# Logits of the last block from gate-times-second-layer weights, its second layer moved into the routing round

## The chip, the cores and the metric

The kernel runs on one core of a Trainium2 chip. The metric is device time in microseconds (us) of one launch. The engines are TensorE (PE, with its weight loads PEld), VectorE (DVE), ScalarE (ACT), GpSimd (POOL), and SyncE (SP), which here issues most of the transfers.

## The reference

Attention over 8 batches and heads of 576 tokens gives x of 4608 tokens by 512. A two-layer network, a gate with a greedy assignment of tokens to 8 experts of 576 places each, and the experts follow:

```python
h = x @ w_in                      # 512 -> 2048
g = h - np.tanh(h)
x = g @ w_out                     # 2048 -> 512
logits = x @ w_gate               # 4608 x 8
flat = logits.flatten()
order = np.argsort(-flat)         # best (token, expert) pairs first
for idx in order:                 # a token takes its best expert that has a place left
    tok, e = (int(idx) // E, int(idx) % E)
    if assigned[tok] >= 0 or counts[e] >= cap:
        continue
    assigned[tok] = e
    counts[e] += 1
for e in range(E):
    mask = assigned == e
    h = np.maximum(x[mask] @ w1[e], 0.0)
    out[mask] = h @ w2[e]
```

All products are made with each operand split into a high and a low part of the fp32r type, three products for one (high by high, low by high, high by low).

## The kernel before, in words

The first part, `phase_ab`, goes over 12 blocks (n = 0 to 11) of 384 tokens. A block has 16 steps (f = 0 to 15), one for each 128 columns of the 2048. From block 2 on the steps come in a fixed order that the loop at the end of `phase_ab` writes out. In step s:

- `h_mm` (L421) gives TensorE 12 products of 128x384 into one of two h banks in PSUM;
- `act1` (L460) gives ScalarE four operations (S, t, T, m) and VectorE four (`act_do`, L448 to L457) that make t = h - tanh h; the last of them frees the h bank;
- `act2` (L473) of the step before splits t into gh (ScalarE) and gl (GpSimd, L471);
- `attn_...` give the attention of a later block, in three parts that take turns by step;
- `logit` (L525) takes a few logits of the block before on VectorE: one operation for each token group of 128 and expert, `scalar_tensor_tensor` of the x2 row and the expert's gate column, summed into a column of L. 24 make a block; the table LOGITS says how many a step takes;
- `x2_mm` (L479) gives TensorE nine products of 128x512 of step s-2 into three x2 banks.

At f = 15, `x_split` splits the attention's result for the next block, half on GpSimd and half on VectorE. After step 15's x2 products `x2_out` (L497) copies the three banks to SBUF and SP stores them to `x2d` in DRAM. Each engine does its queue in the order in which the code gives it instructions.

For block 0, and after the loop for block 11, the logits come from `tlogit` (L534) in place of VectorE: four transposes of the x2 row on TensorE, a copy to SBUF, four fp32 products with the gate, a copy to L.

The second part, `phase_c`, makes eight rounds: a round picks an expert and its tokens (`route`, on VectorE with small products on TensorE), loads that expert's weights, gathers the tokens from `x2d` (GpSimd, L1097), and computes. The round for one expert runs beside the products of the one before; round 0 runs alone. Its first instruction needs all of L; its products (`rt`) need VectorE's comparison (cmp) before each. In it EI is the expert's number and IDX the tokens' places. When EI is known SP loads eight tiles of 256 KB of w1 (`load_w1`, L1059), ScalarE and GpSimd split them (L1074, L1075: w1h, w1l). `run`, near the end, sets what of routing, weights and tokens is given out in which order before the first expert.

Of the kernel before, what the change touches and what calls it, by code (L numbers as in the profile page):

```python
# [39 lines left out]
LOGITS = ((0, 0, 0, 0, 3, 2, 1, 3, 2, 1, 3, 2, 3, 3, 1, 0), (0, 0, 0, 0, 0, 4, 0, 0, 3, 2, 4, 3, 2, 3, 2, 1))  # L40
# [12 lines left out]
MSB = 1  # L53
# [10 lines left out]
PA, PB = C0 / KSC ** 2, C1 / KSC ** 4  # L64

# [61 lines left out]
def moe_kernel(ctx, tc, qkv, wio, wgt, wgk, ident, w1, w2, qtab, vtab, amask, cint, rtf, rti, rth, rtb, out):  # L127
# [5 lines left out]
    L = cpool.tile([128, NCOL, E], F32, name="L")  # L133

    with ExitStack() as bs:
        phase_ab(tc, bs, qkv, wio, wgt, wgk, ident, qtab, vtab, amask, cint, x2d, L)
    with ExitStack() as cs:
        phase_c(tc, cs, w1, w2, rtf, rti, rth, rtb, x2d, L, out)


def phase_ab(tc, ctx, qkv, wio, wgt, wgk, ident, qtab, vtab, amask, cint, x2d, L):
    nc = tc.nc
    wpool = ctx.enter_context(tc.tile_pool(name="wpool", bufs=1))
# [3 lines left out]
    psA = ctx.enter_context(tc.tile_pool(name="psA", bufs=3, space=PSUM))  # L147
    psH = ctx.enter_context(tc.tile_pool(name="psH", bufs=2, space=PSUM))
    psX = ctx.enter_context(tc.tile_pool(name="psX", bufs=3, space=PSUM))
# [130 lines left out]
    def attn_scores():  # L280
# [3 lines left out]
        if early(k):  # L284
            pool, tag = (psX, "x2") if k < 4 and k % 2 == 0 else (psA, "psa")
            PSA[k] = [pool.tile([128, 512], F32, tag=tag, name=f"ps{i}") for i in range(3)]
# [53 lines left out]
    def warm(n):  # L340

        z = bw.tile([128, 512], BF16, tag="S", name="z")
        nc.vector.memset(z, 0.0)
        ps = psX.tile([128, 512], F32, tag="x2", name="warm")
        for _ in range(n):
            nc.tensor.matmul(ps, z[:, :128], z, start=True, stop=True)
# [74 lines left out]
    def h_mm(s):  # L421
        n, f = seq[s]
        h = psH.tile([128, 512], F32, tag="h", name="h")
# [42 lines left out]
    def g_high(s):  # L466
        G[s] = [bw.tile([128, TB], F32R, tag=f"g{i}", name=f"g{i}") for i in "hl"]
# [11 lines left out]
    def x2_mm(s, part=None):  # L479
        n, f = seq[s]  # L480
        if f == 0 and part != 1:
            pool, tag = (psA, "psa") if n == 1 else (psX, "x2")
            X2[n] = [pool.tile([128, DM], F32, tag=tag, name="x2") for _ in range(NT)]
# [13 lines left out]
    def x2_out(n):  # L497
        rs = []
        for i in range(NT):
# [5 lines left out]
            if n >= NB - 2 and i == 1:  # L505
# [4 lines left out]
            if n in (0, NB - 1):  # L510
# [23 lines left out]
    def tlogit(c, r, xT, idm, wk, tp, dve=False):  # L534
# [3 lines left out]
        if dve:  # L538
            nc.vector.tensor_copy(out=xT, in_=tp)
        else:  # L540
            nc.scalar.activation(xT, tp, AF.Copy)
# [4 lines left out]
        nc.vector.tensor_copy(out=L[:, c, :], in_=tp[:, :E])  # L546


# [110 lines left out]
    _, idm, wk = tmp  # L659
    nc.gpsimd.memset(ST[64:], 0.0)  # L660
    PB_ = [psA.tile([128, 512], F32, tag="psa", name=f"pb{i}") for i in range(3)]
# [8 lines left out]
    for s in range(NJ + 2, NS + 2):  # L670
        n, f = seq[s] if s < NS else (NB, s - NS)
        part = au(s)
        if s < NS:
            h_mm(s)
            if n == 2 and f in (3, 5, 8):
                next(tl, None)
                if f == 8:
                    gate(0)
            if n == 2 and f in (2, 4, 7):
                c, r = pl.pop(0)  # L680
                tl = tlogit(c, r, bw.tile([128, DM], F32, tag="junk", name="xT", bufs=1), idm, wk, PB_[2])
                next(tl)
            if f == NF - 1 and n + 1 < NB:
# [13 lines left out]
            if head and f == 1:  # L697
                act2(s - 1)
            act1(s)
        if 1 <= s <= NS and not (s < NS and head and f == 1):  # L700
            act2(s - 1)
        if part == 0:
# [8 lines left out]
        logit((LOGITS[n == 2])[f])  # L711
        if n == NB - 1 and f == 0:
            idm, wk = qt[:, 0, :], qt[:, 1, :KC * E]
            nc.sync.dma_start(out=idm, in_=ident)
            nc.sync.dma_start(out=wk, in_=wgk)
        if s >= 2 and (s >= NS or not head):
            x2_mm(s - 2)
    logit(100)
# [585 lines left out]
```

## Time and profile before

| what | value |
|---|---|
| median of 3 runs | 1524.99 us (1524.97 to 1526.43) |
| the profiled execution | 1528.85 us, of which the span is 1527.0 |
| TensorE busy | 1447.8 us, 95% of the span |
| VectorE busy | 1075.0 us, 70% |
| ScalarE busy | 780.6 us, 51% |
| GpSimd busy | 542.2 us, 36% |

Of 40 equal slices of the span, TensorE is busy 90% or more in all but the first, the last and three around the routing's round 0 (8, 2 and 8 tenths, 954 to 1069 us). The granted clock is at 0.9 or more in every slice but the 27th, from 993 to 1031 us, where it shows 0.5; a slice averages, so the stretch itself is read below. A share says how much of a stage an engine works, and not what the stage waits for: that is read from a stretch's own rows. In the rows "[6.65 <-DVE P L863]" means that the engine was idle for 6.65 us before this instruction, and that what ended it was VectorE's instruction on P of line 863.

### The profile page before, as it was taken

To read this page: it belongs to the slowest core of one execution; us is meant where nothing else is said; L and a number is where in the kernel's file an instruction comes from. 1 tells how busy PE (TensorE), PEld (TensorE's weight loads), DVE (VectorE), ACT (ScalarE), POOL (GpSimd) and SP (SyncE) were. 2 spreads that over 40 slices of the span, in tenths; PEclk is the share of its full clock that TensorE was granted. 3 is DMA by queue.
4 is the path that set the end of the run, shared out by engine and by line. 5 is a ranking of instruction groups with operands and counts; after the bars stand their busy time and mean duration, and the time that the engine had idled before them with its cause. 6 is when DMAs were issued, how large, how long until landed. Compare 5 with 4: busy or idle time off the path is not lost.

```text
span 1527.0 us, 26098 instructions
## 1 busy us (share of the span) xinstructions
PE 1447.8 (95%) x9500; PEld 1271.5 (83%) x9500; DVE 1075.0 (70%) x2682; ACT 780.6 (51%) x1616; POOL 542.2 (36%) x487
## 2 busy tenths in 40 slices
PE   7999999999999999999999999828999999999997
PEld 5787889898989898899888988717788888887996
DVE  5777757787878878788878787777676766765210
ACT  6899965555555646565655555413332323423421
POOL 3555621212222212121222122234544625537541
PEclk9999999999999999999999999959999999999999
DMA  8432131111111111111020100122432432425210
GB/s 280 164 106 97 56 134 70 63 44 62 42 63 42 61 44 42 63 38 67 22 78 27 65 1 21 38 73 72 135 118 87 142 110 81 138 92 186 87 63 32
DMA packets 48609, 122.42 MB, mean 80 GB/s; under 512 B 6624, under 2 KB 13408, under 8 KB 48224
## 3 DMA queue, kind: packets, MB, share of 16 engines
q1 hardware_dynamic: 41184, 99.80, 19.3%
q0 software_dynamic: 6144, 19.93, 4.1%
q8 instruction: 75, 1.23, 0.3%
q10 hardware_dynamic: 1152, 1.02, 0.2%
q14 instruction: 54, 0.44, 0.1%
HBM read 101.85 MB, written 18.87 MB: 79 GB/s over the span
## 4 chain that ended last, share of the span: by engine, by line
PE 75%; ACT 8%; DVE 7%; issue 4%; DMA 2%; POOL 2%; SPq 0%; POOLq 0%; ACTq 0%; DVEq 0%
PE x L490 22%; PE h L427 21%; PE ff L1189 12%; PE ff L1158 11%; PE pb L291 2%; PE pb L358 2%; PE pb L370 1%; DMA wst<-in_wio 1%; ACT wst L213 1%; ACT t L440 1%; PE tp L1112 1%; ACT wst L218 1%; PE pb L306 1%; POOL w2l L1075 1%; DVE t L451 1%
## 5 line engine op out<-in xcount | busy, mean ns | idle before, releaser
L471 POOL TENSOR_TENSOR gl<-t,gh 128x384 fp32r<-128x384 f32 x192 | 197.2, 1027 | 633.1 <-ACT gh L468 566.3
L427 PE MATMUL h<-xh,w0h 128*128 128x384 f32 x704 | 238.6, 339 | 1.8 <-DVE t L457 1.8
L437 ACT ACTIVATE S<-h 128x384 f32<-128x384 f32 x192 | 93.4, 487 | 283.4 <-PE h L427 283.4
L427 PE MATMUL h<-xh,w0l 128*128 128x384 f32 x704 | 236.8, 336 | 0.0
L490 PE MATMUL x<-w1h,gh 128*128 128x512 f32 x576 | 232.0, 403 | 2.7 <-ACT gh L468 2.7
L490 PE MATMUL x<-w1l,gh 128*128 128x512 f32 x576 | 227.1, 394 | 0.2 <-DVE w1l L238 0.2
L490 PE MATMUL x<-w1h,gl 128*128 128x512 f32 x576 | 217.3, 395 | 1.4 <-POOL gl L471 0.8
L451 DVE SCALAR_TENSOR_TENSOR t<-t,S 128x384 f32<-128x384 f32 x192 | 114.2, 595 | 141.1 <-ACT t L440 140.3
L531 DVE SCALAR_TENSOR_TENSOR junk<-x2r,wg 128x512 f32<-128x512 f32 x240 | 167.0, 696 | 5.1
L427 PE MATMUL h<-xl,w0h 128*128 128x384 f32 x704 | 151.7, 336 | 0.3 <-DVE xl L414 0.3
L427 PEld LDWEIGHTS h<-xh,w0h 128*128 128x128 f32 x704 | 131.9, 187 | 11.5 <-DVE t L457 3.3
L1075 POOL TENSOR_TENSOR w2l<-ws,w2h 128x512 fp32r<-128x512 f32 x64 | 82.5, 1291 | 163.7 <-ACT w2h L1074 163.7
L427 PEld LDWEIGHTS h<-xh,w0l 128*128 128x128 f32 x704 | 132.1, 188 | 7.1
L490 PEld LDWEIGHTS x<-w1h,gl 128*128 128x128 f32 x576 | 108.4, 189 | 29.1 <-POOL gl L471 5.7
L1189 PE MATMUL ff<-w2h,hh 128*128 128x512 f32 x320 | 128.1, 400 | 3.1 <-DVE hl L1171 2.0
L490 PEld LDWEIGHTS x<-w1h,gh 128*128 128x128 f32 x576 | 108.5, 188 | 26.0 <-ACT gh L468 4.0
L457 DVE COPY_PREDICATED t<-m,h 128x384 f32<-128x384 uint16 x192 | 114.5, 596 | 21.3 <-ACT m L446 2.6
L1189 PE MATMUL ff<-w2l,hh 128*128 128x512 f32 (+1 forms) x320 | 128.0, 400 | 0.6 <-POOL w2l L1075 0.6
L440 ACT ACTIVATE t<-S,bias 128x384 f32<-128x384 f32 x192 | 118.2, 616 | 17.1 <-POOL gl L471 1.1
L427 PEld LDWEIGHTS h<-xl,w0h 128*128 128x128 f32 x704 | 125.7, 188 | 0.9 <-DVE xl L414 0.9
L490 PEld LDWEIGHTS x<-w1l,gh 128*128 128x128 f32 x576 | 108.6, 189 | 17.8 <-DVE w1l L238 0.5
L1158 PE MATMUL ff<-xh,w1h 128*128 128x288 f32 x512 | 115.5, 304 | 6.4 <-DVE hl L1171 5.5
(210 smaller groups left out, 2935.3 us busy)
## 6 DMA issues: line engine op xcount, KB each, us to landing
ws<-in_w SPq DMA_DIRECT2D x128, 256.0 KB, 2.9
ain<-in_qkv SPq DMA_DIRECT2D x36, 768.0 KB, 4.1
wst<-in_wio SPq DMA_DIRECT2D x32, 512.0 KB, 3.5
x2d<-x2r SPq DMA_DIRECT2D x33, 256.0 KB, 2.0
w1h<-in_qkv SPq DMA_DIRECT2D x12, 192.0 KB, 4.8
w1l<-in_qkv SPq DMA_DIRECT2D x12, 192.0 KB, 3.5
w0h<-in_qkv SPq DMA_DIRECT2D x12, 192.0 KB, 4.5
w0l<-in_qkv SPq DMA_DIRECT2D x12, 192.0 KB, 4.3
```

What stands on the lines that cost most here:

```text
L291: nc.tensor.matmul(PSA[k][a][:, chunk(c)], kt[r, chunk(c)], q[r, chunk(c)], start=True, stop=True)
L427: nc.tensor.matmul(h[:, :TB], w[0][f][:, hp, :], x, start=i == 0, stop=i == 11)
L437: nc.scalar.activation(S, h, AF.Square, scale=KSC)
L440: nc.scalar.activation(AT[s][2], AT[s][1], AF.Square, bias=bias[:, 0:1])
L451: nc.vector.scalar_tensor_tensor(t, t, PA - PB * PB / 4, S, op0=OP.add, op1=OP.mult)
L457: nc.vector.copy_predicated(t, m.bitcast(U16), h)
L471: nc.gpsimd.tensor_tensor(G[s][1], TT.pop(s), G[s][0].bitcast(F32), op=OP.subtract)
L490: nc.tensor.matmul(X2[n][i], g[:, i * 128:i * 128 + 128], w, start=(f == 0 and g is gh and w is wh), stop=(f == NF - 1 and g is gl))
L531: nc.vector.scalar_tensor_tensor(j, r, 1.0, wg[e // 4][:, e % 4, :], op0=OP.mult, op1=OP.mult, accum_out=L[:, c, e:e + 1])
L1075: nc.gpsimd.tensor_tensor(l, s, h.bitcast(F32), op=OP.subtract)
L1158: nc.tensor.matmul(ps[u], w[:, k, :], x[:, k, 288 * u:288 * u + 288], start=i == 0, stop=i == 11)
L1189: nc.tensor.matmul(o, h, w, start=f == 0 and i == 0, stop=f == 7 and i == len(prods) - 1, skip_group_check=t == 4)
```

## The change

Logits are x2 times the gate, and x2 is g times w_out. The new kernel makes WP = w_out times gate (2048 x 8) while earlier blocks run, and takes the logits of the last block as g times WP, without its x2. The x2 of that block is still needed by the gathers, and its products are given out later.

- WP. Its 16 pieces are one for each f. Ten pieces are made on VectorE (`w_gate`, eight operations a piece, placed by the table GATES in steps f = 14, 15 and 0 to 3 from block 2 on), from a sum of the high and low weight tiles that GpSimd makes (`w_add`). Six pieces (WPE) are made by TensorE in blocks 3 to 8: GpSimd's sum `wt` at f = 12, four transposes right behind h of f = 13, a copy on ScalarE, four fp32 products at f = 14, and a copy. In block 10 WP is split in two parts, WPS.
- Last block, from f = 2. `logit_mm` gives three products of 72x384 a step, of step s-3, into one bank. Three h banks take turns in place of two. x2 products are taken from a generator (`x2_rest`, 144 products): 17 by FILL0 in the block, 23 by FILL1 behind it, and the remaining ones by FILL2 in round 0, ahead of the routing's products. The g tiles stay in the places of weights that are no longer used.
- Block 10's logits: two token groups by `tlogit` in the last block, the third by eight operations on VectorE.
- The last logits are copied (lT), transposed three times and copied to L.
- The copies of the last x2 are all on ScalarE, and its stores on SP come behind the loads of w1.
- The routing's tables are loaded in block 2 and its state is copied in block 11. Pools of PSUM become fixed banks, and the weights of `phase_c` take the places of earlier tiles.

The core of the diff:

```diff
-LOGITS = ((0, 0, 0, 0, 3, 2, 1, 3, 2, 1, 3, 2, 3, 3, 1, 0), (0, 0, 0, 0, 0, 4, 0, 0, 3, 2, 4, 3, 2, 3, 2, 1))
+LOGITS = ((0, 0, 0, 0, 3, 2, 1, 3, 2, 1, 3, 2, 3, 3, 1, 0), (0, 0, 0, 0, 0, 4, 0, 0, 3, 2, 4, 3, 2, 3, 2, 1),
+          (0, 0, 0, 0, 1, 1, 1, 1, 1, 1, 1, 1, 0, 0, 0, 0))
+WPE = 10, 11, 12, 13, 14, 15
+GATES = 1, 3, 2, 1, 0, 0, 0, 0, 0, 0, 0, 0, 0, 0, 2, 2
+FILL0 = 0, 0, 0, 0, 1, 1, 1, 1, 1, 1, 2, 2, 2, 2, 2, 1
+FILL1 = 2, 8, 6, 4, 2
+FILL2 = 3, 7, 2, 2, 2, 6, 0, 9, 0, 9, 0, 10, 0, 9, 0, 9, 0, 9, 7, 10, 5, 8, 200
...
-        h = psH.tile([128, 512], F32, tag="h", name="h")
+        h = bank((3, 4, 1)[f % 3] if n == NB - 1 else 3 + s % 2, "h")
...
+    def w_add(o, f):
+
+        h, l = (w[1][f].rearrange("p k m -> p (k m)").bitcast(F32) for w in (WH, WL))
+        nc.gpsimd.tensor_tensor(o, h, l, op=OP.add)
+
+    def w_gate(k):
+
+        f, e = divmod(k, E)
+        j = bw.tile([128, DM], F32, tag="junk", name="junk", bufs=1)
+        nc.vector.scalar_tensor_tensor(j, wsum, 1.0, wg[e // 4][:, e % 4, :], op0=OP.mult, op1=OP.mult,
+                                       accum_out=WP[:, k:k + 1])
+
+    def logit_mm(s, part):
+
+        f = seq[s][1]
+        gh, gl = G[s]
+        for i, g in ((0, gh), (1, gh)) if part == 0 else ((0, gl),):
+            nc.tensor.matmul(lg[:MG, :TB], WPS[:, i, E * f:E * f + MG], g, start=f == 0 and part == i == 0,
+                             stop=f == NF - 1 and part == 1)
+
+    def x2_rest():
+
+        n, s0 = NB - 1, NS - NF
+        X2[n] = [bank(i + 5, "x2") for i in range(NT)]
+        order = [(f, i) for f in range(NF - 3) for i in range(NT)]
+        order += [(f, i) for i in range(NT) for f in range(NF - 3, NF)]
+        for f, i in order:
+            gh, gl = G[s0 + f]
+            wh, wl = (w[1][f].rearrange("p k m -> p (k m)") for w in (WH, WL))
+            for j, (g, w) in enumerate(((gh, wh), (gh, wl), (gl, wh))):
+                nc.tensor.matmul(X2[n][i], g[:, i * 128:i * 128 + 128], w, start=f == j == 0, stop=f == NF - 1 and j == 2)
+                if f == NF - 1 and j == 2:
+                    c = n * NT + i
+                    r = wpool.tile([128, DM], F32, tag=TAGS[32 + i], name="x2r")
+                    nc.scalar.activation(r, X2[n][i], AF.Copy)
+                    nc.sync.dma_start(out=x2d[c * 128:c * 128 + 128, :], in_=r)
+                yield
...
+            if n - 3 in range(len(WPE)) and f in (13, 14):
+                if f == 13:
+                    tl = tlogit(WP[:, E * wf:E * wf + E], wt, wt, idm, wk, PB_[2])
+                next(tl, None)
...
+            if end:
+                if f == 2:
+                    lg = bank(2, "lg")
+                if f >= 3:
+                    logit_mm(s - 3, 0)
+                    logit_mm(s - 3, 1)
+                fill(FILL0[f])
...
+        if NG < nd and (n, f) > (2, 12):
+            for _ in range(GATES[f]):
+                w_gate(NG)
+                NG += 1
+                if NG % E == 0:
+                    due = NG < nd
+                    break
+        if n - 3 in range(len(WPE)) and f == 12:
+            wf = WPE[n - 3]
+            wt = ap_.tile([128, 2, 3, 128], F32, tag="ms", name="wt", bufs=MSB).rearrange("p a c t -> p (a c t)")[:, :DM]
+            w_add(wt, wf)
...
-    tls = [tlogit(c, r, xT, idm, wk, PB_[i], i != 1) for i, ((c, r), xT) in enumerate(zip(pl, spare))]
-    for _ in range(2):
-        for t in tls:
-            next(t, None)
+    for i, k in enumerate(FILL1[:3]):
+        fill(k)
+        logit_mm(NS - 3 + i, 0)
+        if i == 2:
+            fill(FILL1[3])
+        logit_mm(NS - 3 + i, 1)
+    lT = sp[:MG, 2 * DM:2 * DM + TB]
+    nc.scalar.activation(lT, lg[:MG, :TB], AF.Copy)
+    fill(FILL1[4])
...
     def run(i, done):
         while not done():
             next(threads[i][1])
+            if i == 0:
+                fill_(next(pauses, 0))
```

TensorE's queue in block 3 at f = 13, with the change: h's last products (L449), the transposes of wt (L562), x2 of step 11 (L515).

```order
L449 MATMUL h<-xl,w0h_1760 128x384 x4
L562 MATMUL pb_2271<-tab_65,wt 128x128 [waits DMAHW2_49,DVE_49,Pool_49]
L562 MATMUL pb_2271<-tab_65,wt 128x128 x3
L515 MATMUL x_3233<-w1h_1703,gh 128x512 [waits Activation_49]
L515 MATMUL x_3233<-w1l_1710,gh 128x512
```

Before, x2 of step 11 followed h directly; the transposes now stand between, and wait for GpSimd.

TensorE's queue where the last block ends, before: products of `tlogit` (L544) and then the routing's first products (L930).

```order
L544 MATMUL pb_2268<-qt,xT 128x8 [waits DMAHW3_49,DVE_49]
L544 MATMUL pb_2268<-qt,xT 128x8 x3
L544 MATMUL pb_2269<-qt,xT 128x8 [waits Activation_49]
L544 MATMUL pb_2269<-qt,xT 128x8 x3
L544 MATMUL pb_2270<-qt,xT 128x8 [waits DVE_49]
L544 MATMUL pb_2270<-qt,xT 128x8 x3
L930 LDWEIGHTS cmp_10375 [waits DVE_49,PE_49]
L930 MATMUL rt<-P,cmp_10375 128x32 [waits DVE_49]
```

And with the change: the last logit product (L588), the transposes of lT (L850), then 22 x2 products (L601), of which the first and the last stand here, and the routing's first product (L1053).

```order
L588 MATMUL lg<-gl,wps 72x384 [waits Pool_49]
L601 MATMUL x_10006<-w1l_950,gh 128x512
L601 MATMUL x_10006<-w1h_932,gl 128x512
L850 MATMUL lt<-tab_65,sp 128x72 [waits DVE_49,Activation_49]
L850 MATMUL lt<-tab_65,sp 128x72 x2
L601 MATMUL x_10007<-w1h_932,gh 128x512
...
L601 MATMUL x_10008<-w1h_1159,gh 128x512
L1053 LDWEIGHTS cmp_10501 [waits DVE_49,PE_49]
L1053 MATMUL rt<-P,cmp_10501 128x32 [waits PE_49]
```

The x2 products that stood ahead of the logits now stand behind them, ahead of the routing's.

SP's queue in round 0, with the change: the last two loads of w1 (L1186), the three stores of the last block's x2 (L606), then the loads of w2 (L1191).

```order
L1186 DMA ws<-in_w 128x512 [waits DMAHW0_49]
L1186 ISA
L1186 DMA ws<-in_w 128x512 [waits DMAHW1_49]
L606 DMA x2d<-x2r 128x512 [waits DMAHW2_49,Activation_49]
L606 DMA x2d<-x2r 128x512 [waits DMAHW3_49,Activation_49]
L606 DMA x2d<-x2r 128x512 [waits DMAHW4_49,Activation_49]
L1191 ISA
L1191 DMA ws_11092<-in_w 128x512 [waits DMAHW5_49,PE_49,Pool_49]
```

Before, these stores stood ahead of all eight loads.

## Rows read from the trace of the kernel before

**Rows 1.** Windows: start:end, length; busy us of PE, PEld, DVE, ACT, POOL; clock, DMA.

```profile
300.00:400.00 100.00, 99.94 (x628) 89.99 (x627) 78.48 (x190) 55.87 (x120) 22.88 (x22) 1.00 0.14 48
992.00:1028.00 36.00, 7.42 (x132) 5.89 (x133) 27.31 (x84) 3.62 (x6) 10.90 (x5) 0.50 0.15 50
0.00:34.00 34.00, 26.74 (x286) 19.21 (x286) 18.57 (x47) 21.00 (x41) 9.14 (x12) 1.00 0.91 309
```

**Rows 2.** Timeline of block 5, steps 12 and 13: start, us, engine, line, operation.

```profile
506.13 0.34 PE L427 MATMUL h<-xh,w0h 128*128 128x384 f32 x1
508.25 0.39 PE L490 MATMUL x<-w1h,gh 128*128 128x512 f32 x1
510.32 0.34 PE L427 MATMUL h<-xh,w0h 128*128 128x384 f32 x1
506.89 1.01 POOL L471 TENSOR_TENSOR gl<-t,gh 128x384 fp32r<-128x384 f32 x1 [6.15 <-ACT gh L468]
505.49 0.56 DVE L451 SCALAR_TENSOR_TENSOR t<-t,S 128x384 f32<-128x384 f32 x1 [1.45 <-ACT t L440]
507.78 0.67 DVE L531 SCALAR_TENSOR_TENSOR junk<-x2r,wg 128x512 f32<-128x512 f32 x1
```

**Rows 3.** Timeline and chain of waits from the last block's step 2 to the routing.

```profile
920.02 0.34 PE L427 MATMUL h<-xh,w0h 128*128 128x384 f32 x1
975.06 2.10 PE h L427 x12
981.55 1.02 POOL L471 TENSOR_TENSOR gl<-t,gh 128x384 fp32r<-128x384 f32 x1 [0.73 <-POOL gl L471]
984.68 1.51 PE L537 MATMUL pb<-qt,x2r 128*128 128x128 f32 x12
986.06 2.85 PE L544 MATMUL pb<-qt,xT 128*128 128x8 f32 x24
990.57 0.46 DVE L823 TENSOR_REDUCE st<-L 128x36 f32<-128x288 f32 x1 [1.46 <-ACT st L812]
```

**Rows 4.** Timeline of PE in the first routing round.

```profile
995.55 0.40 PE L930 MATMUL rt<-P,cmp 128*128 128x32 bf16 x9 [6.65 <-DVE P L863]
999.08 0.42 PE L930 MATMUL rt<-P,cmp 128*128 128x32 bf16 x9 [2.42 <-DVE cmp L925]
1019.51 0.24 PE L995 MATMUL rt<-X,tb 128*128 128x72 bf16 x1 [1.95 <-DVE ei L990]
1025.53 1.23 PE L1027 MATMUL rt<-R,A 128*128 128x160 bf16 x8 [5.72 <-ACT R L1019]
```

**Rows 5.** Timeline of SP, ACT and POOL between the expert's number and its products.

```profile
1020.71 4.07 SPq L1063 DMA_DIRECT2D ws<-in_w  x8
1024.60 0.88 ACT L1019 ACTIVATE R<-b,tf 128x720 bf16<-128x720 bf16 x1
1028.53 2.01 ACT L1074 ACTIVATE w1h<-ws 128x512 fp32r<-128x512 f32 x3 [0.21 <-DMA ws<-in_w]
1028.68 1.14 POOL L1097 DMA_INDIRECT xg<-x2d,idx  x1 [2.09 <-DVE st L832]
1034.87 7.41 POOL L1075 TENSOR_TENSOR w1l<-ws,w1h 128x512 fp32r<-128x512 f32 x6
```

**Rows 6.** Timeline of POOL and DVE where a gl meets two logits.

```profile
265.42 1.32 POOL L471 TENSOR_TENSOR gl<-t,gh 128x384 fp32r<-128x384 f32 x1 [5.51 <-ACT gh L468]
265.17 0.69 DVE L531 SCALAR_TENSOR_TENSOR junk<-x2r,wg 128x512 f32<-128x512 f32 x1
265.91 1.38 DVE L531 SCALAR_TENSOR_TENSOR junk<-x2r,wg 128x512 f32<-128x512 f32 x1
```

**Rows 7.** Page, part 6: transfers, KB each, median us from issue to landing.

```profile
x2d<-x2r SPq DMA_DIRECT2D x33, 256.0 KB, 2.0
```

**Rows 8.** Timeline of PE at the lower clock: x2 products of the first steps.

```profile
36.15 0.63 PE L490 MATMUL x<-w1h,gh 128*128 128x512 f32 x1
36.58 0.63 PE L490 MATMUL x<-w1l,gh 128*128 128x512 f32 x1
```

More of the change, by code (lines that the diff above doesn't have):

```diff
@@ L284, in attn_scores @@
         if early(k):
-            pool, tag = (psX, "x2") if k < 4 and k % 2 == 0 else (psA, "psa")
-            PSA[k] = [pool.tile([128, 512], F32, tag=tag, name=f"ps{i}") for i in range(3)]
+            PSA[k] = [bank(i + (5 if k < 4 and k % 2 == 0 else 0), f"ps{i}") for i in range(3)]
         q, kt, _, _ = AIN[k]
@@ L481, in x2_mm @@
         if f == 0 and part != 1:
-            pool, tag = (psA, "psa") if n == 1 else (psX, "x2")
-            X2[n] = [pool.tile([128, DM], F32, tag=tag, name="x2") for _ in range(NT)]
+            X2[n] = [bank(i + (0 if n == 1 else 5), "x2") for i in range(NT)]
         gh, gl = G[s]
@@ L545, in tlogit, with fill @@
                              stop=k == KC - 1)
-        nc.vector.tensor_copy(out=L[:, c, :], in_=tp[:, :E])
+        nc.vector.tensor_copy(out=o, in_=tp[:, :E])
+    def w_add(o, f):
[28 more added lines that the diff above has]
+                yield
+    def fill(k):
+        for _ in range(k):
+            next(rest, None)
     warm(WARM)
@@ L658, in phase_ab @@
     nx["scale"] = nx["load"] - 2
[L659 removed]
     nc.gpsimd.memset(ST[64:], 0.0)
[L661 removed]
+    PB_ = [bank(i, f"pb{i}") for i in range(3)]
     PSA.update((k, PB_) for k in range(4 * NA0, len(pairs)))
@@ L668, in au @@
         return i % 3 if 0 <= i < 12 else None
-    for s in range(NJ + 2, NS + 2):
+    NG, due, wsteps, lag = 0, False, {}, 0
+    nd = E * (NF - len(WPE))
+    (ti, _), (tf, _), _, _ = tables
+    idm = tf[:, RF["id"][0]:RF["id"][1]]
+    rest = x2_rest()
+    for s in range(NJ + 2, NS + 1):
         n, f = seq[s] if s < NS else (NB, s - NS)
         part = au(s)
+        end = n == NB - 1 and f > 1
         if s < NS:
@@ L710, in phase_ab @@
                 attn_load()
[L711 to L716, printed above, removed]
+        logit(LOGITS[0 if n < NB - 1 else 2][f] if n != 2 else LOGITS[1][f])
+        if (n, f) == (2, 12):
+            w_add(wsum, 0)
+        if NG < nd and (n, f) > (2, 12):
[5 more added lines that the diff above has]
+                    break
@@ L717, in phase_ab @@
+        if s >= 2 and s < NS and not head and not end:
             x2_mm(s - 2)
+        if (n, f) == (NB - 1, 12):
+            st = bank(0, "st")
+            nc.scalar.activation(st[:, :RF["bank"][1] - RF["bank"][0]], tf[:, RF["bank"][0]:RF["bank"][1]], AF.Copy)
     logit(100)
-    spare = [ap_.tile([128, 4, TB], F32, tag="ain", name="xT").rearrange("p a t -> p (a t)") for _ in range(2)]
-    spare = [spare[i // 2][:, i % 2 * DM:i % 2 * DM + DM] for i in range(NT)]
-    tls = [tlogit(c, r, xT, idm, wk, PB_[i], i != 1) for i, ((c, r), xT) in enumerate(zip(pl, spare))]
@@ L722, in phase_ab @@
-    for _ in range(2):
-        for t in tls:
-            next(t, None)
+    for i, k in enumerate(FILL1[:3]):
[7 more added lines that the diff above has]
+    fill(FILL1[4])
+    lt = bank(1, "lt")
+    for i in range(NT):
+        nc.tensor.transpose(lt[:, MG * i:MG * i + MG], lT[:, 128 * i:128 * i + 128], idm[:MG, :MG])
@@ L728 @@
+    nc.vector.tensor_copy(out=L[:, (NB - 1) * NT:, :], in_=lt[:, :NT * MG].rearrange("p (c e) -> p c e", e=MG)[:, :, :E])
+    return st, fill
 BIG = 1e38
@@ L811, in phase_c @@
     nc.gpsimd.memset(sc, 0.0)
-    nc.scalar.activation(bank[:, :203], F["bank"], AF.Copy)
     EI, IDX = {}, {}
```

134 lines of the change are left out of this document (84 added, 50 removed).

## The prediction

> **What bounds the kernel now.** I read four views in this order: busy time by stretch, to find the bound of each stage; the timelines of one middle block on three engines; the end of the layer and the chain into the routing; the first routing round up to the first expert product. The reader is to see two different stages. In the blocks TensorE is busy 99.94 of 100 us at a granted clock of 1.00, with VectorE at 78.5 and ScalarE at 55.9 [rows 1]: a product added there costs its length, and so does a wait of TensorE. In the first routing round TensorE is busy 7.42 of 36 us at a clock of 0.50 (1.2 GHz), while VectorE is busy 27.31 [rows 1]: that stage is a chain through VectorE, and TensorE has room. The change takes products out of the first place and puts them into the room of the second, and pays for it with other work in the first.
>
> All sums stand against the profiled execution, 1528.85 us (span 1527.0). It lies 3.9 us above the median of the runs, 1524.99; I take the difference to be the same for both kernels and add the sum to the median.
>
> **Prices.** In block 5 the 12 h products of a step start at 506.13, its nine x2 products at 508.25, the next step at 510.32 [rows 2]: an h group is 2.12 us (0.177 a product of 384 columns), an x2 product 2.07/9 = 0.23. A logit product also streams 384 columns, so I price it as an h product; three of them are 0.53.
>
> **Part 1, the last block and its tail.** Before, h of step 2 starts at 920.02 and the last h group at 975.06; GpSimd's last gl ends at 982.57, the x2 products end at 984.7, and three sets of transposes, copies and products follow; the routing's first instruction starts at 990.57, after a last wait of 1.46 for ScalarE's copy of its state [rows 3]. After, TensorE has from 920.02 to the end of the last h group: 14 h groups (29.7), 12 logit groups (6.4), 16 x2 products (3.7) and two sets of block 10's logits by transposes. One set costs 1.38/3 = 0.46 for the transposes (984.68 to 986.06) and 2.85/3 = 0.95, with handing-over, for the products [rows 3]; I take 1.36 and 2.7 for both. That ends at 962.5. Then 21 x2 products (4.8) and the other 12 logit products (2.1): 969.4. The last gl is hidden by them: it ended 5.4 us behind the last h group (977.16 to 982.57, [rows 3]), and here 6.8 us lie between that group and the product that reads it. Behind them come a copy on ScalarE, three transposes and the copy to L. No row has the first at its size; before, three sets of transposes, copies and products took 4.4 (984.68 to 990.57, less the wait of 1.46, [rows 3]), or 1.5 a set, and one such pass with less in it I take at 1.4: routing starts at 970.8. **-19.8 us.** The table wait is part of it. VectorE needs 2.29 for the four activation operations of a step (505.49 to 507.78, [rows 2]) and 0.74 for one logit: 3.0 a step against TensorE's 2.9 to 3.1, so it is nearly level, which is a rival below.
>
> **Part 2, the 105 x2 products left for the routing.** 22 stand ahead of the first routing product (5.1 us), where TensorE waited 6.65, 5.0 of it after the routing's start; then nine or ten (2.1 to 2.3) ahead of groups that waited some 2.4 (999.08), and 21 (4.8) ahead of the one that waited 5.72 [rows 4]. At 0.23 each they fit, with 0.1 to 0.9 to spare: nothing, and the routing products run at the higher clock. Off each of nine groups (0.40 to 0.42 for nine products at the lower clock) I take 0.07, an estimate: **-0.6** (between -1.5 and +1.0, the latter if each group's fill is late by 0.1).
>
> **Part 3, the product of the second weights and the gate.** The six pieces on TensorE in blocks 3 to 8 cost 6 x 1.36 = **+8.2**; ScalarE's copy (0.6) and VectorE's (0.1) hide beside h products. But their transposes stand right behind the 12 h products of step 13 in TensorE's queue, and wait for a sum of two tiles that GpSimd makes behind gl(11). In block 5 gl(11) runs from 506.89 to 507.90 and h(13) is done at 508.25 [rows 2]. An operation of that size takes GpSimd 7.41/6 = 1.24 [rows 5]. If it starts at 507.95, TensorE waits to 509.25, with a hand-over, 1.0 us, with x2(11), which is ready, queued behind. VectorE has three logits in this step, the first from 507.78 [rows 2], and the two engines get in each other's way: at 265.42 a gl that starts inside a logit takes 1.32 in place of 1.01, and the next logit 1.38 in place of 0.69 [rows 6]. So GpSimd would wait to about 508.35 (that gl lost 0.31, to 0.56 after the logit's start) and end at 509.6: a stall of 1.4 with the hand-over. I take that, since it is the row nearest to it; the bounds are 1.0 and 1.5. **+8.6** (6.0 to 9.0). VectorE's late logits (by 1.3) lie under TensorE's own stall.
>
> The ten other pieces are 80 operations like a logit on VectorE, 0.69 each and 0.74 apart [rows 6], 59 us over some eight blocks, 7 us a block. A block's 16 steps are at least 67 us (4.19 each, [rows 2]), of which VectorE idles 21.5 in 100 [rows 1], or 14. They stand in steps 14, 15 and 0 to 3, which hold few or no logits. What is late next is the release of an h bank: step 12's activations end at 507.78, 5.8 us after its products began (506.13 less 4.19), and the bank is wanted two steps, 8.4 us, after that, so 2.5 us are spare, of which the three operations of one step take 2.2. I take **+0.5**, between 0 and 4 (0.5 a block). The tables' loads moved to SP in block 2 lie beside a DMA share of 0.14 [rows 1]: nothing. The split of the sums and the copy of the routing's state are one operation each on engines with idle time: nothing.
>
> **Part 4, the three stores of x2.** They moved on SP's queue from ahead of the round's eight weight loads to behind them, and the five gathers on GpSimd, which need x2, now wait for them; behind the gathers in GpSimd's queue stand six weight subtractions, and behind all of it the first expert product. Before, the expert's number is there at 1019.5 [rows 4], the eight loads are issued from 1020.71 to 1024.78, ScalarE splits the last three of them from 1028.53 to 1030.54, and the first gather starts at 1028.68, held by its index alone [rows 5]. After, counted from the expert's number, ScalarE can copy x2 only behind R (done at +6.0, [rows 5]), so the stores are issued by +7.9. A store lands 2.0 us after its issue when nothing is ahead of it [rows 7]: +9.9, against +9.2 for the gather: a delay of 0.7. If they wait for the eight loads, whose last is there at about +9.4, and need three transfers' time (0.7 to 0.8 each: the loads, issued 0.5 apart, are used over 1023.4 to 1029.9), they land at +12: a delay of 2.8 to 3.3. I take **+2.8**, because the loads before it on that queue already land one after the other; bounds 0.7 and 3.3. The delay reaches the end, for the experts' products fill TensorE from there on.
>
> The Trainium skill, "DMA: Bandwidth & Descriptors", section "Queues, rings and completion order", says that a DMA engine takes its descriptors in ring order and that a semaphore's increment lands only after every earlier write of that engine. By that rule the stores cannot be reported ahead of the loads, and the delay is the upper one; no row here has a store behind loads, so nothing shows it yet, and by the bare row of a store the sum would be 2.1 lower.
>
> **Sum.** -19.8 - 0.6 + 8.2 + 8.6 + 0.5 + 2.8 = -0.3: 1528.55 for a profiled execution, **1524.7 us** by the median.
>
> **The rivals.** *The two waits cost less.* GpSimd's sum starts at 507.90 (6.0 in place of 8.6) and the stores land at +9.9 (0.7 in place of 2.8): -5.0, 1520.0. With no stall at all at step 13, the sum is -11.0 and the time 1514. For it: the logit at 507.78 begins 0.12 before gl(11) ends, and neither is longer than others [rows 2]. Against it: the lengthened pair [rows 6], and one queue for loads and stores.
> *VectorE becomes the bound of the last block.* There gl (1.0) falls on every 2.9 us, with VectorE busy throughout; where it meets a logit, VectorE loses 0.7 (1.38 against 0.69, [rows 6]). In the eight steps with a logit that is up to 5.6, and VectorE already needs 3.0 of about 3.0: 1530.3. Five of the eight steps must be hit before it is slower by 0.2%. Against it: gl follows ScalarE's gh, which is queued so that it falls beside VectorE operations that read h.
> *The clock stays at 0.50 in the routing round.* An x2 product then takes 0.43 (36.15 to 36.58, [rows 8]) and a fill of nine 3.9 against a wait of 2.4: 1.5 for each of seven groups, 4.4 for the 22 and 3.3 for the 21: some 18, 1543. Three such stages are enough for slower. Against it: in the first 34 us TensorE is busy 26.74 of 34 and keeps 1.00 [rows 1], and with the fills a stage is about as busy.
> That the x2 products do not leave the path at all is excluded by their place: routing's first product needs L, which no longer needs x2.
>
> **How the numbers follow.** Forecast (within 0.2%, some 3 us, about what a measurement can tell from no change): 0.45. The waits cost less: 0.33, nearly all of it faster by more than that. VectorE the bound, in the last block or in the blocks with the 80 operations: 0.16. Clock: 0.06. That gives faster 0.33, same 0.45, slower 0.22. The range leaves out the case without any stall, the clock case and the end of the VectorE case: 1517.5 to 1531.
>
> **What would show it.** Step 1: the routing's first reduction 19.8 earlier, corrected by the stalls ahead of it. Step 3: TensorE idle 1.0 to 1.5 before the first transpose of step 13 in six blocks, released by GpSimd. Step 4: the first gather waiting for a DMA, 12 us after the expert's number. Step 2: the routing products waiting on VectorE and not on x2, at a clock of 1.00. The forecast is wrong if the routing starts less than 15 earlier net of the blocks, or if TensorE's share falls below 99% in the blocks other than at step 13.

## The result, and the profile after

The changed kernel takes 1540.38 us (median of 4 runs, 1539.16 to 1540.91) against 1525.32 for the kernel before in the same comparison: 1.0096 of it, 95% interval 1.0079 to 1.0114. It is 15 us slower. Forecast were 1524.7 and a range up to 1531.

The profiled execution of the change is 1540.91 us with a span of 1539.1, 12.1 longer than the span before. Where the 12.1 came from, by the start of the same event in both traces (h groups of the last block, the routing's first reduction, the first gather, the first expert product, the end):

| stretch | changed less before, us | forecast |
|---|---|---|
| up to block 2, step 12 | +1.7 | 0 |
| from there to the last block's step 2 | **+30.3** | +17.3 |
| last block from step 2, to the routing's first reduction | -20.4 | -19.8 |
| routing round 0, to the expert's number | -0.5 | -0.6 |
| from there to the first gather | +3.9 | +2.8 |
| first gather to first expert product | -1.0 | 0 |
| first expert product to the end | -2.1 | 0 |

The first row holds nothing of the change: over the traces of the runs below it lies between -2.0 and +3.2 against the same trace of the kernel before. All sums below are counted from block 2, step 12.

Busy time by stretch, after, first a stretch of the blocks and then the routing round (columns as in [rows 1]):

```profile
300.00:400.00 100.00, 98.47 (x639) 87.30 (x640) 93.94 (x214) 56.01 (x117) 28.13 (x25) 1.00 0.13 48
1004.00:1040.00 36.00, 29.80 (x232) 21.83 (x231) 27.52 (x86) 4.58 (x9) 10.95 (x5) 1.00 0.19 61
```

Against [rows 1] the round is what was hoped for: TensorE busy 29.8 of 36 us in place of 7.4, at 1.00 in place of 0.50, and VectorE at the same 27. In the blocks TensorE has lost 1.5 of 100 us, and VectorE has gone from 78.5 to 93.9.

The routing's products after, from the timeline; where [rows 4] has waits of 6.65 and 2.42, 0.25 is left, and VectorE is still what ends it:

```profile
1007.29 0.38 PE L1053 MATMUL rt<-P,cmp 128*128 128x32 bf16 x9 [0.25 <-DVE P L986]
1010.71 0.39 PE L1053 MATMUL rt<-P,cmp 128*128 128x32 bf16 x9 [0.25 <-DVE cmp L1048]
```

VectorE's waits between 300 and 400 us (engine and line, what it waited for, total us, times, longest), first before, then after. This is the row that the prediction should have rested on: before, all idle time but the gaps of a few tenths is seven waits of up to 3.1 us for ScalarE's t; after, none is left.

```profile
DVE t L451 <- ACT t L440: 16.3, 7, 3.1
```

```profile
DVE t L473 <- ACT t L462: 0.9, 2, 0.5
```

Groups of VectorE (operation, count | busy us, mean ns | idle before). The first activation operation of a step (L473) took 595 ns before and takes 749 now, a logit (L556) 696 and 783; the new operations (L580) take 860 in place of the 0.69 us of [rows 6]. The second activation operation (L475), which has h in PSUM as an input, is not longer. The first two lines are of before (L451 and L531 there), the others of after:

```profile
L451 DVE SCALAR_TENSOR_TENSOR t<-t,S 128x384 f32<-128x384 f32 x192 | 114.2, 595 | 141.1 <-ACT t L440 140.3
L531 DVE SCALAR_TENSOR_TENSOR junk<-x2r,wg 128x512 f32<-128x512 f32 x240 | 167.0, 696 | 5.1
L473 DVE SCALAR_TENSOR_TENSOR t<-t,S 128x384 f32<-128x384 f32 x192 | 143.8, 749 | 58.1 <-ACT t L462 58.0
L556 DVE SCALAR_TENSOR_TENSOR junk<-x2r,wg 128x512 f32<-128x512 f32 x224 | 175.4, 783 | 4.7
L475 DVE TENSOR_TENSOR t<-t,h 128x384 f32<-128x384 f32 x192 | 106.3, 554 | 21.9 <-ACT T L465 4.5
L580 DVE SCALAR_TENSOR_TENSOR junk<-wsum,wg 128x512 f32<-128x512 f32 x80 | 68.8, 860 | 2.0
```

The edge of a block after, from the timelines of three engines (step 15 of block 5). GpSimd's split of the next block's input and its gl stand beside two of the new operations and the first activation operation of the step; each of these VectorE operations takes twice its time alone or more, and a later h group of TensorE waits for the end of that chain, which frees its bank:

```profile
533.83 2.45 POOL L436 TENSOR_TENSOR xl<-xf,xh 128x384 fp32r<-128x384 f32 x2 [1.51 <-PE h L449]
533.84 1.56 DVE L580 SCALAR_TENSOR_TENSOR junk<-wsum,wg 128x512 f32<-128x512 f32 x1
535.44 1.39 DVE L580 SCALAR_TENSOR_TENSOR junk<-wsum,wg 128x512 f32<-128x512 f32 x1
537.31 1.34 POOL L497 TENSOR_TENSOR gl<-t,gh 128x384 fp32r<-128x384 f32 x1 [1.03 <-PE h L449]
537.70 1.36 DVE L473 SCALAR_TENSOR_TENSOR t<-t,S 128x384 f32<-128x384 f32 x1
540.94 0.44 PE L449 MATMUL h<-xh,w0h 128*128 128x384 f32 x1 [0.36 <-DVE t L479]
```

And the stall at step 13 that was forecast, TensorE's transposes of wt in the same block, with GpSimd's sum ahead of it:

```profile
522.19 1.60 POOL L574 TENSOR_TENSOR wt<-w1h,w1l 128x512 f32<-128x512 f32 x1
523.84 0.66 PE L562 MATMUL pb<-tab,wt 128*128 128x128 f32 x4 [1.27 <-POOL wt L574]
```

All of TensorE's longer waits after, from block 2, step 12, to the last block's step 2 (what it waited for, total us, times, longest). At the edges TensorE waits not only for the chain that frees a bank (t) but also for VectorE's half of the split of the next block's input (xl), 2.6 of the 3.4 us in step 0 of block 3:

```profile
PE pb L562 <- POOL wt L574: 6.6, 6, 1.3
PE h L449 <- DVE t L479: 4.4, 10, 1.8
PE h L449 <- DVE xl L436: 3.4, 3, 1.8
```

### The profile page after: what moved, and what is told of

Same layout as the page of the kernel before. It is cut to its first block, busy times and chain, and to the rows that moved or that the text cites. A ratio compares the mean times of both kernels' runs of the same rounds, so it can differ in the third digit from the quotient of the medians.

```text
span 1539.1 us, 26476 instructions
## 1 busy us (share of the span) xinstructions
PE 1473.4 (96%) x9611; PEld 1280.8 (83%) x9611; DVE 1169.1 (76%) x2814; ACT 791.6 (51%) x1626; POOL 575.9 (37%) x504
## 4 chain that ended last, share of the span: by engine, by line
PE 39%; DVE 12%; issue 2%; ACT 1%; DMA 1%; POOL 1%; POOLq 0%; DVEq 0%; ACTq 0%
PE ff L1311 12%; PE ff L1280 12%; PE h L449 6%; PE x L515 4%; DVE junk L556 2%; PE tp L1234 1%; DVE t L473 1%; DVE t L479 1%; DVE t L475 1%; DVE junk L580 1%; DVE h L477 1%; PE x L601 1%; PE lg L588 1%; DVE cmp L1048 1%; PE rt L1057 0%
## 5 line engine op out<-in xcount | busy, mean ns | idle before, releaser
L497 POOL TENSOR_TENSOR gl<-t,gh 128x384 fp32r<-128x384 f32 x192 | 205.4, 1070 | 607.2 <-ACT gh L494 531.9
L449 PE MATMUL h<-xh,w0h 128*128 128x384 f32 x704 | 240.4, 342 | 6.1 <-DVE t L479 4.8
L449 PE MATMUL h<-xh,w0l 128*128 128x384 f32 x704 | 236.6, 336 | 0.0
L515 PE MATMUL x<-w1h,gh 128*128 128x512 f32 x528 | 214.3, 406 | 2.5 <-ACT gh L494 2.0
L515 PE MATMUL x<-w1l,gh 128*128 128x512 f32 x528 | 208.5, 395 | 0.2 <-DVE w1l L261 0.2
L515 PE MATMUL x<-w1h,gl 128*128 128x512 f32 x528 | 199.2, 397 | 0.2 <-POOL gl L497 0.2
L473 DVE SCALAR_TENSOR_TENSOR t<-t,S 128x384 f32<-128x384 f32 x192 | 143.8, 749 | 58.1 <-ACT t L462 58.0
L556 DVE SCALAR_TENSOR_TENSOR junk<-x2r,wg 128x512 f32<-128x512 f32 x224 | 175.4, 783 | 4.7
L449 PE MATMUL h<-xl,w0h 128*128 128x384 f32 x704 | 154.0, 338 | 3.5 <-DVE xl L436 3.4
L449 PEld LDWEIGHTS h<-xh,w0h 128*128 128x128 f32 x704 | 131.9, 187 | 23.1 <-DVE t L479 15.7
L449 PEld LDWEIGHTS h<-xh,w0l 128*128 128x128 f32 x704 | 132.2, 188 | 6.2
L449 PEld LDWEIGHTS h<-xl,w0h 128*128 128x128 f32 x704 | 125.6, 188 | 6.6 <-DVE xl L436 6.6
L475 DVE TENSOR_TENSOR t<-t,h 128x384 f32<-128x384 f32 x192 | 106.3, 554 | 21.9 <-ACT T L465 4.5
L468 ACT ACTIVATE m<-S,bias 128x384 bf16<-128x384 f32 x192 | 116.5, 607 | 8.9 <-DVE t L479 8.8
L515 PEld LDWEIGHTS x<-w1h,gl 128*128 128x128 f32 x528 | 100.0, 190 | 24.5 <-POOL gl L497 3.1
```

The source lines that it names most:

```text
L449: nc.tensor.matmul(h[:, :TB], w[0][f][:, hp, :], x, start=i == 0, stop=i == 11)
L468: nc.scalar.activation(AT[s][4], AT[s][1], AF.Relu, bias=bias[:, 1:2])
L473: nc.vector.scalar_tensor_tensor(t, t, PA - PB * PB / 4, S, op0=OP.add, op1=OP.mult)
L475: nc.vector.tensor_tensor(t, t, h, op=OP.mult)
L497: nc.gpsimd.tensor_tensor(G[s][1], TT.pop(s), G[s][0].bitcast(F32), op=OP.subtract)
L515: nc.tensor.matmul(X2[n][i], g[:, i * 128:i * 128 + 128], w, start=(f == 0 and g is gh and w is wh), stop=(f == NF - 1 and g is gl))
```

## The experiments

Two theories stood against each other. **A**: the 80 operations for ten of the pieces have made VectorE the bound of the blocks. **B**: TensorE's wait at step 13 and what it drags behind it cost the blocks their time, and VectorE only follows. In the table "blocks" is the growth from block 2, step 12, to the last block's step 2 against the kernel before, from the traces; the ratio is to the kernel before on the same chip.

| run | blocks, us | median, us | ratio (95%) |
|---|---|---|---|
| the change | +30.3 | 1540.38 | 1.0096 (1.0079 to 1.0114) |
| e1, no VectorE operations | +16.5 | 1525.16 | 1.0000 (0.9990 to 1.0009) |
| e2, one sum only | +30.2 | 1538.99 | 1.0086 (1.0069 to 1.0103) |
| e3, early sum | +34.1 | 1543.14 | 1.0117 (1.0100 to 1.0134) |
| e4, stores on ScalarE's queue | +30.2 | 1543.14 | 1.0114 (1.0097 to 1.0131) |
| e5, operations in idle steps | +23.5 | 1533.02 | 1.0028 (1.0007 to 1.0050) |
| e6, x2 ahead of the round | +30.3 | 1556.81 | 1.0200 (1.0182 to 1.0218) |
| e7, idle steps and early sum | **+9.3** | 1518.94 | 0.9953 (0.9937 to 0.9970) |
| e8, pieces on TensorE | +20.3 | 1530.19 | 1.0022 (1.0012 to 1.0033) |
| e9, e7 with early stores | +9.5 | 1516.60 | 0.9925 (0.9909 to 0.9942) |
| e10, stores ahead of the loads | +9.2 | 1520.14 | 0.9959 (0.9944 to 0.9975) |
| e11, stores on GpSimd, R first | +9.1 | 1516.84 | 0.9949 (0.9936 to 0.9963) |

**e1: without the VectorE operations and their sums.**

```diff
-    nd = E * (NF - len(WPE))
+    nd = 0
+    nc.gpsimd.memset(WP, 0.0)
...
-        if (n, f) == (2, 12):
-            w_add(wsum, 0)
```

> The changed kernel without the 80 operations on VectorE for ten pieces of the product of gate and second weights, and without the ten GpSimd sums before them; those pieces are zero, so the last block's logits lack them. Theory A (VectorE has become the bound of the blocks, since these operations and GpSimd's hold each other up): the 14.3 us that the blocks lost beyond TensorE's own work come back, so about 1526 us, and VectorE's first activation operation falls from 749 ns back to about 600. Rival B (the loss is TensorE's wait at step 13 and what it drags behind it, VectorE only follows): under 2 us come back, 1538.5 or more.

The blocks gave back 13.8 us and the median 15.2 (to 1525.16); theory A's number, and B is out. Each of the six blocks with a piece on TensorE now grows by 2.7 to 2.9 and nothing else does: 1.9 at step 13 (the stall and the transposes) and 0.9 at step 14 (the products). Of what came back, 11.3 lay in steps 0 to 2 of the blocks. VectorE's first activation operation is back at 594 ns, with 141 us of idle time before it in all:

```profile
L473 DVE SCALAR_TENSOR_TENSOR t<-t,S 128x384 f32<-128x384 f32 x192 | 114.1, 594 | 141.2 <-ACT t L462 140.8
```

**e2: only the first of the ten sums.**

```diff
             due = False
-            w_add(wsum, NG // E)
```

> The changed kernel with the 80 operations on VectorE kept, but only the first of the ten GpSimd sums that feed them (all read the first sum, so nine pieces are wrong). Theory A with mutual blocking as its larger half: each sum left out gives back 0.4 to 0.7 us, in all 4 to 6, 1534 to 1536 us. Theory A by the mere number of VectorE operations: under 1.5 us, 1539 or more. Rival B: no change.

The blocks are the same to 0.1 us, and the first activation operation still takes 749 ns:

```profile
L473 DVE SCALAR_TENSOR_TENSOR t<-t,S 128x384 f32<-128x384 f32 x192 | 143.8, 749 | 55.9 <-ACT t L462 55.8
```

So it is not the other nine sums that lengthen VectorE's operations. What is left beside the 80 operations, and seen beside them at the edge above, is gl and the split of x, which were there before. The first sum, which this run keeps, is another matter: step 13 of block 2, where it runs, is 1.1 us longer in every run that makes it, and not in e1.

**e3: TensorE's pieces summed one step earlier.**

```diff
-        if n - 3 in range(len(WPE)) and f == 12:
+        if n - 3 in range(len(WPE)) and f == 11:
```

> The changed kernel with GpSimd's sum for each of TensorE's six pieces given out one step earlier (step 11 in place of 12), so that the transposes of step 13 find it ready. If VectorE is the bound (A), TensorE's wait of 1.3 goes in six blocks but VectorE's lateness fills part of it: 3 to 8 us back, 1532 to 1537. If the wait itself is the cause (B), all of 8 and what follows it, 8 to 14 back, 1526 to 1532.

Neither theory's number: the blocks became 3.8 us slower. The wait at the transposes is gone, but the same time and more is waited at the block's edge, for VectorE. The first h groups of blocks 4, 5 and 6 that wait for a bank (step 0 or 1), from TensorE's timeline:

```profile
369.72 0.41 PE L449 MATMUL h<-xh,w0h 128*128 128x384 f32 x1 [1.50 <-DVE t L479]
457.75 0.44 PE L449 MATMUL h<-xh,w0h 128*128 128x384 f32 x1 [0.86 <-DVE t L479]
536.91 0.41 PE L449 MATMUL h<-xh,w0h 128*128 128x384 f32 x1 [1.53 <-DVE t L479]
```

Over the same stretch as above TensorE's waits for this chain are 10.1 us in place of 4.4, and those for VectorE's half of the split 8.5 in place of 3.4. The stall had been giving VectorE time to catch up. And a sum at step 11 takes 1.64 to 1.77 us in place of 1.29, where it meets VectorE. That is A in a stronger form than I had stated it.

**e5: the same 80 operations in other steps.** By the timelines of before, VectorE stood idle, in the mean of blocks 3 to 10, for 3.4 us in step 0, 3.1 in 2, 2.4 in 5, 1.8 in 8 and 1.6 in 11, and for 0.2 to 0.5 in every other one (a step here from one first activation operation to the next).

```diff
-GATES = 1, 3, 2, 1, 0, 0, 0, 0, 0, 0, 0, 0, 0, 0, 2, 2
+GATES = 3, 0, 3, 0, 0, 2, 0, 0, 2, 0, 0, 1, 0, 0, 0, 0
```

> The changed kernel with the same 80 VectorE operations in other steps: three in step 0, three in 2, two in 5, two in 8, one in 11, where VectorE of the kernel before stood idle for 3.3, 3.1, 2.4, 1.8 and 1.7 us, in place of steps 14, 15 and 0 to 3. If their place at the block's edge is what costs (theory A1), most of the 13.8 us goes and the time is 1528 to 1532. If VectorE simply has no room for 11 operations a block once it meets GpSimd (A2), they cost as much wherever they stand: 1537 or more.

1533.02, a ratio of 1.0028: the blocks gave back 6.8, half of the 13.8 and not yet most of it. At the edge of the blocks hardly anything is left. Of the 7.0 that remain beside the pieces on TensorE (23.5 against e1's 16.5), 1.1 stand in block 2 behind the first sum, and 5.6 lie in two blocks, 5 and 8, where a sum for VectorE now falls due at step 12 too, just ahead of TensorE's, and the stall doubles:

```profile
515.46 1.27 POOL L574 TENSOR_TENSOR wsum<-w1h,w1l 128x512 f32<-128x512 f32 x1
516.69 1.74 POOL L574 TENSOR_TENSOR wt<-w1h,w1l 128x512 f32<-128x512 f32 x1
518.48 0.66 PE L562 MATMUL pb<-tab,wt 128*128 128x128 f32 x4 [2.48 <-POOL wt L574]
```

**e7: e5 with e3's early sum.** Both edits together.

> The 80 operations placed as in the run before the last one and GpSimd's sum for TensorE's six pieces given out at step 11 in place of 12. Theory A1: with VectorE no longer late, the stall of 1.4 in six blocks goes too, 8 us below the run with the moved operations alone: 1520 to 1524, at or below the kernel before. A2: the sum at step 11 meets VectorE again, as it did with the old places, and nothing or less is won.

1518.94, 0.9953 of the kernel before, a little better than the range: the edit that cost 3.8 us in e3 is worth 14 here. The blocks grow by 9.3. The six pieces, at 0.45 in step 13 and 0.9 in step 14, are 8.1 of it (8.2 by the bare price), and 1.1 stand in block 2 behind the first sum: 0.2 are left for the 80 operations. TensorE is back at its share of [rows 1], with VectorE at 87 (the stretch first), and its first activation operation and the new ones are at 625 and 691 ns (the grouped view behind it):

```profile
300.00:400.00 100.00, 99.94 (x632) 90.04 (x632) 87.06 (x218) 55.50 (x119) 25.53 (x25) 1.00 0.14 48
```

```profile
L473 DVE SCALAR_TENSOR_TENSOR t<-t,S 128x384 f32<-128x384 f32 x192 | 120.0, 625 | 76.4 <-ACT t L462 75.7
L580 DVE SCALAR_TENSOR_TENSOR junk<-wsum,wg 128x512 f32<-128x512 f32 x80 | 55.3, 691 | 2.5
```

VectorE's whole busy time says the same by the page: 1068.1 us without the 80 operations (e1), 1124.0 with them in idle steps (e7), 1169.1 where the change put them. To add the same work costs VectorE 56 us in one place and 101 in the other; these sums hold also what its other operations were lengthened.

**e8: fifteen pieces on TensorE, two a block, and one on VectorE in block 3.** The sums are given out two steps ahead of the transposes (steps 10 and 12 for 12 and 14).

> Fifteen pieces on TensorE, two a block in blocks 3 to 9 and one in block 10, at steps 12 to 15, each behind a GpSimd sum given out two steps earlier, and one piece as eight operations on VectorE in block 3. If TensorE's work is the bare price of a piece (1.36 us) and a sum two steps early causes no wait: 21 us in place of the 30 that the blocks lost, 1530 to 1533. If the pieces at steps 14 and 15, beside the split of the next block's input, make VectorE late again: 1536 or more.

1530.19. The blocks grow by 20.3, which is 1.35 a piece: the price from [rows 3] holds in the mean. It is made up of unlike parts: steps 12 to 15 of a block with two pieces grow by 2.7 to 3.1, step 0 of the blocks gives back 0.3 to 1.0, and block 2, with the first sum, adds 2.7.

**e6: all x2 products ahead of the round.**

```diff
-FILL2 = 3, 7, 2, 2, 2, 6, 0, 9, 0, 9, 0, 10, 0, 9, 0, 9, 0, 9, 7, 10, 5, 8, 200
+FILL2 = 200,
```

> The changed kernel with all 105 x2 products that are left ahead of the routing round's first product, in place of between its products. If the round hides them (the prediction's part 2), the first routing product comes (105 - 22) x 0.23 = 19 us later, less the 4 us by which the gathers waited for the stores, which now lie ahead of the weight loads: 15 us slower than the change, 1555. If the round does not hide them, the time stays at 1540.

The first routing product comes 23.5 us behind the routing's first reduction in place of 5.1, 18.4 later, and from that reduction to the end it takes 551.6 in place of 536.8: 14.7 us. The round hides what it was said to hide. The rest of the 18.4 comes back at the gathers: the stores, now issued ahead of the loads, land in 2.0 us each, and the first gather starts 9.7 us after the expert's number, held by its index alone as before.

**e4: the three stores on ScalarE's queue.**

```diff
-                    nc.sync.dma_start(out=x2d[c * 128:c * 128 + 128, :], in_=r)
+                    nc.scalar.dma_start(out=x2d[c * 128:c * 128 + 128, :], in_=r)
```

> The changed kernel with the three stores of the last block's x2 issued from ScalarE's queue in place of SP's, where they stand behind the eight weight loads. If the stores wait behind the loads in SP's rings, the first gather starts 2 to 3.5 us earlier counted from the expert's number: 1537 to 1538.5. If they wait for the transfer engines as a whole, or for ScalarE's copies, nothing: 1540.

No gain: the first gather starts 15.4 us after the expert's number, against 13.3 in the change and 9.3 before. The stores were issued from +7.8 to +9.8 (+7.5 to +8.5 in the change) and landed later, not earlier. Their landing (minimum, median, maximum over the three) in the change, and here:

```profile
DMA to landing us min/median/max: 3.6/3.8/3.9
```

```profile
DMA to landing us min/median/max: 4.6/4.7/5.1
```

**e9: e7, with the last 21 x2 products, their copies and the stores right behind the expert's number, on ScalarE's queue.**

```diff
     run(0, lambda: 0 in EI)
+    next(threads[0][1])
+    fill_(200)
     run(1, lambda: len(W1) == 2)
```

(with a pause in `route` behind the products of X, and the store of e4)

> The kernel with moved VectorE operations and the early sums, and with the last 21 x2 products given out right behind the two products that follow the expert's number, their three copies on ScalarE ahead of the first weight splits, and the stores from ScalarE's queue. If the gathers came 4 us late because the stores were issued late, behind ScalarE's splits and R (+7.6 from the expert's number), they are issued from +2 to +6.5 here and the gathers come at +10 in place of +13.9: 3 to 4 us faster than the kernel without this, 0.9930 to 0.9935 of the kernel before. If the transfer engines, busy with 2 MB of weights, are what delays them, the gathers still come at +12 or later: 0.9945 or more.

The gathers came at +14.4, so the mechanism missed; that the ratio is about the one that it would have given is luck. The stores were issued at +1.8, +3.9 and +7.5 (the last of them 1.6 us after its copy, for it waited for the landing of a weight load with which it shares a semaphore), but landed in 3.2 to 6.1 us; the weights came later, and R, which stands behind the first two splits on ScalarE, and with it the index, came 2.9 us later than in e7. The time, 1516.60, lies below e7's, but on another chip; from the routing's first reduction to the end it is 536.0 against 537.7, and not by way of the gathers: the 1.7 lie behind the first expert product. The intervals of the two ratios overlap.

**e10: the same with the stores on SP's queue, ahead of the loads.**

> As the other run of this call, but the stores stay on SP's queue, where they now stand ahead of the eight weight loads, which so wait for the last of x2 (+6.5 from the expert's number in place of +1.2). The gathers come at +9.5, held by the index alone, but the first weight split comes 5 us later. If the weights have room before the first expert product, 4 us faster than without: 0.9930. If the splits on GpSimd, two of them ahead of the gathers in its queue, hold the gathers in turn, they come at +14 or later: no gain, 0.9950 or more.

The stores, with no load ahead of them, landed in 2.0 to 2.4 us. Gathers at +16.0, held by an index that came 5.8 us later than in e7, behind weights that were loaded late; 0.9959, no gain over e7, as the second case had it.

**e11: the stores on GpSimd's queue, R ahead of all splits, and the splits on GpSimd behind the gathers.**

> The kernel with moved VectorE operations and early sums; the last 21 x2 products and their copies right behind the expert's number, as in the two runs before; the stores from GpSimd's queue, ScalarE's R ahead of all weight splits, and all GpSimd splits of the first weights behind the gathers. If R and the index, pushed back by ScalarE's splits, were what took the gain away there, the index comes at +9, the stores land by then, and the gathers come at +9 to +10.5 from the expert's number: 3 to 4 us faster than the kernel with moved operations and early sums alone, 0.9925 to 0.9935 of the kernel before. If the stores land late beside the weight loads in any case: gathers at +12 or later, 0.9945 or more.

The index came at +8.9 as expected; the gathers came at +13.0 all the same. The last store, issued at +6.2, landed about 6 us later (minimum, median, maximum of the three):

```profile
DMA to landing us min/median/max: 4.1/5.6/5.9
```

On three queues a store beside the eight weight loads, or behind them, takes 3.2 to 6.1 us where it takes 2.0 alone [rows 7] and 2.0 to 2.4 ahead of them (e6, e10). What counts is when it is issued, and not on which queue: in e9 and e11, from two other queues, each store landed within 0.7 us of the load that was issued just before it (in e9 at +5.1, +9.4 and +13.6, those loads at +4.4, +9.1 and +13.4). The transfer engines had 2 MB of weights to move, and a store waited for what had been issued ahead of it. The ratio, 0.9949, is e7's within the intervals.

## Why the prediction was wrong

**Part 1 held.** The last block and its tail gave 20.4 for 19.8. From step 7 on the h groups there follow each other at 2.83 to 3.09 us, as TensorE's sum had it (in steps 3 to 6, with block 10's logits, at 3.1 to 3.7), and TensorE is busy without a gap from 952 to 994 us: VectorE kept up, and that rival did not come.

**Part 2 held.** The round gave 0.5 for 0.6, TensorE's waits there ended by VectorE but for one of 1.8 for ScalarE's R, at a granted clock of 1.00; e6 shows what the hiding is worth. (Of the 144 x2 products 39 are given out before the round, 17 by FILL0 and 22 by FILL1, not 23; the 105 are right.) The clock rival did not come.

**The stall and the six pieces held.** 15.9 for 16.8 in the change (the growth at steps 13 and 14 of the six blocks); e1 gives 2.8 a block there against 1.36 + 1.4. GpSimd's sum is not late as I had it, but starts right behind gl and takes 1.72 to 1.75 us (e1) in place of 1.24; its end is where I put it.

**The ten pieces on VectorE are the step that failed.** I took +0.5 and a bound of 4; with their sums they cost 13.8 (e1), of which the first sum alone is 1.1. Three things were wrong in it. I compared 7 us a block with the 14 that VectorE idled, an average over a hundred microseconds, though its idle time stood in five steps out of sixteen, and none of them was 14, 15, 1 or 3. I took the spare of an h bank from the middle of a block, step 12, and used it at the edge, where the split of x and an activation chain already follow each other without a gap. And I priced an operation at its time alone, while the row that I used for the stall [rows 6] said that an operation beside GpSimd takes twice that. With the operations in the idle steps and TensorE's sums a step earlier (e7) the 80 operations cost some 0.2 us, so the mechanism was the place, not the number. How much of the 13.8 is the lengthening beside GpSimd, and how much the want of idle time in these steps alone, no run separates: moving the operations took away both. I had named VectorE as a rival, but in the last block by name and with a price for the eight logits there; in the blocks only as an aside, at 0.5 a block.

**Part 4 was right in kind and too small in size.** 3.9 for 2.8, above my upper bound of 3.3. The last store landed at +12.4, for the +12 that I had; what I left out is the 0.9 us that the first gather starts behind that landing (0.8 to 0.9 also in e4, e9 and e11). The reason that I gave, the queue, was not shown: the stores land as late from other queues (e4, e9, e11), and on time only when they are issued ahead of the loads (e6, e10). By the Trainium skill, "DMA: Bandwidth & Descriptors", section "Issuing engines are not separate DMA queues", transfers of all issuing engines run on the same transfer engines and interleave; these runs agree, 3.2 to 6.1 us for a store against 2.0. Of the two rules that the prediction cited from the same page of the Trainium skill, ring order alone would have let a store on another queue pass, and it did not pass; that an increment lands only behind every earlier write fits the rows.

**Not foreseen and not settled:** from the first expert product to the end the changed kernels take 1.8 (e5, e7) to 3.7 us (e10) less than the kernel before; the change takes 2.1 less. The place can be read: from the last expert product to the end it is 9.3 us in the one trace of before and 5.6 to 5.7 in all twelve others, 3.6 to 3.7 less; up to the last product the changed kernels take none to 1.9 us more. The cause is open: no run bears on it, and with one trace of before it may lie in that execution alone. Nor is it settled why the median moved by 15.1 when the profiled executions moved by 12.1; the two profiled executions lie 3.5 and 0.5 above their medians.

## What to carry to other kernels

Before work is moved to an engine that "has 20% idle", list its waits by step: idle time in five lumps of 1.6 to 3.4 us a block takes eleven operations only in those lumps, and a table of places is worth as much as the change itself (1.0096 and 0.9953 are the same kernel with one table and one step number altered). Price the operation beside the neighbour that it will meet, not alone. And when a wait is taken away and the time gets worse, as in e3, another engine had been living on that wait.

## What the runs showed of the hardware

VectorE and GpSimd hold each other up by nearly whole operations. In the change a first activation operation alone takes 0.53 to 0.56 us, a logit or a new operation 0.67 to 0.69; of those that overlap an operation of GpSimd some take over twice that, up to 1.64 and 1.75. GpSimd's sum takes up to 1.77 in place of 1.29 (e3). In [rows 6] a logit, a gl and a logit, 0.69, 1.01 and 0.69 alone, take 2.12 from the first's start to the last's end. Over a kernel this made 45 us of VectorE's busy time out of waiting (101 against 56). The Trainium skill, "SBUF — State Buffer", section "SBUF: two separate sides", says that an operation of VectorE with two SBUF inputs and one of GpSimd that reads SBUF lock a shared pair of ports for a whole instruction; the rows agree: the operation of the same chain that has one input in PSUM keeps its 554 ns, and the 84 of them that overlap an operation of GpSimd take no more than 0.56 us.
